# Weight-chunk bounds from TensorE column sums of the magnitude words, instead of a ScalarE pass with an accumulator

## The chip, the cores and the metric

The kernel runs on one core of one Trainium2 chip. The metric is the device time of one execution in microseconds (us); lower is better. Before the change, three runs gave 757.84, 759.58 and 761.88 us, median 759.58.

Names used below: TensorE (PE, with its weight loads as PEld), VectorE (DVE), ScalarE (ACT), GpSimd (POOL), SyncE (SP, which here only issues DMAs).

## The reference

Attention with a bias that a small network makes from positions, followed by a gated feed-forward block. Inputs are float32 for q, k, v and the bias network, and float64 for the three feed-forward weights.

```python
# B, H, S, D = 4, 8, 576, 64; d_model 512, d_ff 1536
scores = q @ k.T / sqrt(D) + bias(positions; w1, b1, w2)     # per batch and head
attn = softmax(scores)
x = (attn @ v) as [B * S, H * D]                             # 2304 x 512
out = ((x @ w_a) * (x @ w_b)) @ w_out
```

## The kernel before

**What runs.** For each batch, head pair and group of 256 query rows the kernel makes scores on TensorE (`qk`), adds the bias and takes the row minimum of the negated scores on VectorE (`soft1`, L518), takes exp with a row sum on ScalarE (L523), forms the reciprocal of the sum (GpSimd L567, VectorE L568), scales the rows on GpSimd (L573), transposes them on TensorE into PSUM (`turn`, L585), copies that to SBUF on ScalarE (L590, L595) and multiplies with v on TensorE (L535, L613). The feed-forward blocks (`moe_block`, L715, and `moe_out`, L764) run in 256-token pieces. The first feed-forward piece needs w_a and w_b as scaled pairs of float16 matrices, so in the first 160 us of the program attention tiles and weight preparation run side by side.

**Weight preparation.** w_a and w_b are cut into 12 chunks each of 128 x 512 float64 values: 24 chunks, taken in turn a, b, a, b, and handled in six groups of four. Step `s` of `wab_steps` (L318) does the following.

- `wab_conv` for chunk `s`: `w_unit` (L261) turns the two 32-bit halves of each float64 into a float32. ScalarE scales the upper half (L264); VectorE shifts (L266) and merges the lower half (L267), which leaves the *magnitude word*, the float32 without its sign, in `u`. `u` lies in the SBUF space where the float16 pair of that chunk will stand later (`w16t[:, f, j]`). VectorE then puts the sign in (L270) and the result goes to a float32 tile `wt`.
- `wab_size` for chunk `s-1` (L281): ScalarE passes over the signed float32 chunk with Abs and an accumulator, which leaves the sum of magnitudes of each of the 128 partitions in one column of `wm`. Its elementwise output lands in `w16t` and is overwritten later.
- Every fourth step, `pow2_down` (L75) turns the four columns of `wm` into four powers of two: a TensorE matmul against the identity brings them to four partitions (L77), VectorE takes the maximum over 128 elements (L79), clamps it (L80), keeps the exponent (L81) and spreads it on a diagonal (L85). Two steps later `pow2_up` broadcasts them to all partitions (TensorE L90, VectorE L92), and `wab_scale` makes reciprocals (L293, L294).
- `wab_parts` for chunk `s-7`: GpSimd scales the chunk (L304), ScalarE casts it to float16 (L307), GpSimd subtracts to get the lower part (L308).

**What sets the order.** TensorE's instructions run in the order of the code: the calls of `merge` interleave attention steps, weight steps and feed-forward steps, and a weight step's matmul stands where that step is called. The other engines' queues are ordered by a scheduler with a cost model; every engine works its queue in order. SP issues in order too: the load of a weight chunk (`wraw`, L258, three buffers in each of two pools) waits for the VectorE merge (L267) that frees its buffer, and the loads of bias rows and v behind it wait with it. PSUM banks matter at one place: the transposes of one tile (`tp`, one buffer) wait for ScalarE's copy of the tile before.

To keep the TensorE clock up in early stretches, `keep(n)` issues n matmuls whose result nobody reads (L845, 128 x 512 float16).

Of the kernel before, what the change touches and what calls it, by code (L numbers as in the profile page):

```python
# [8 lines left out]
F32 = mybir.dt.float32  # L9
F32R = mybir.dt.float32r  # L10
F16 = mybir.dt.float16
BF16 = mybir.dt.bfloat16
I32 = mybir.dt.int32
AF = mybir.ActivationFunctionType
ALU = mybir.AluOpType
AX = mybir.AxisListType
# [10 lines left out]
KC = DM // 128  # L27
# [25 lines left out]
def attention_moe(ctx, tc, q0d, q1d, kd, vd, idn, wp, wa, wb, wo, lsw, lg, rl, out):  # L53
    nc = tc.nc
# [14 lines left out]
    def pr_tile():  # L69
        if prp[0]:  # L70
            return prp[0].tile([128, 512], F32, tag="pr", name="pr", bufs=1)
        return mps.tile([128, 2 * TOK], F32, tag="ab", name="pr", bufs=3)


    def pow2_down(mx, n, tag):  # L75
        ps = pr_tile()
        nc.tensor.matmul(ps[0:n, 0:128], mx, tab["idn"], start=True, stop=True)  # L77
        m = wtp[1].tile([n, 1], F32, tag="p2m" + tag, name="p2m", bufs=2)
        nc.vector.reduce_max(out=m, in_=ps[0:n, 0:128], axis=AX.X)  # L79
        nc.vector.tensor_scalar(out=m, in0=m, scalar1=3.0e38, scalar2=2.0 ** -100, op0=ALU.min, op1=ALU.max)  # L80
        nc.vector.tensor_scalar(  # L81
            out=m.bitcast(I32), in0=m.bitcast(I32), scalar1=0x7F800000, scalar2=None, op0=ALU.bitwise_and
        )
        dg = wtp[1].tile([n, n], F32, tag="p2d" + tag, name="p2d", bufs=2)
        nc.vector.tensor_scalar(out=dg, in0=tab["idn"][0:n, 0:n], scalar1=m, scalar2=None, op0=ALU.mult)  # L85
        return dg

    def pow2_up(dg, n, tag):
        ps = pr_tile()
        nc.tensor.matmul(ps[:, 0:n], tab["one"][0:n, :], dg, start=True, stop=True)  # L90
        g = wtp[1].tile([128, n], F32, tag="p2g" + tag, name="p2g", bufs=2)
        nc.vector.tensor_copy(g, ps[:, 0:n])  # L92
        return g
# [9 lines left out]
    tab = {}  # L103
# [18 lines left out]
    def bias_windows(pool, tag):  # L122
        u = pool.tile([128, S], F32, tag=tag, name="u", bufs=1)
        nc.sync.dma_start(out=u, in_=lsw)
        return u
# [63 lines left out]
    @contextmanager  # L189
    def late():  # L190
        with ExitStack() as s:
            for x in (ttrs, exps, evs, pns):
                if x:
                    s.enter_context(tc.issue_after(x[-1].ins))
            yield
# [57 lines left out]
    last, wtp = [], [None, None]  # L253
# [21 lines left out]
    w16, wos, gpool = {}, {}, [None]  # L275
# [3 lines left out]
        with late():  # L279
            return w_unit(wt, raw, w16t[:, n // 2, n % 2].rearrange("p x k n -> p (x k n)").bitcast(I32))  # L280

    def wab_size(f, j, wf, m):
        nm = "ab"[j]
        w16[nm, f] = w16t[:, f, j]
        c = 2 * (f % 2) + j
        with late():
            nc.scalar.activation(
                w16[nm, f][:, 0], wf.rearrange("p (k n) -> p k n", k=KC), AF.Abs, accum_out=m[:, c:c + 1]
            )

    def wab_scale(p, m):
        rm = wtp[1].tile([128, 4], F32, tag="rm", name="rm", bufs=2)
        nc.vector.reciprocal(out=rm, in_=m)  # L293
# [4 lines left out]
        return rm  # L298

    def wab_parts(p, c, wf, rm):  # L300
        w = w16["ab"[c % 2], 2 * p + c // 2]
        wv = wf.rearrange("p (k n) -> p k n", k=KC)
        hi, lo = w[:, 0], w[:, 1]
        nc.gpsimd.tensor_scalar(  # L304
            out=wv, in0=wv, scalar1=rm[:, c:c + 1], scalar2=PS, op0=ALU.mult, op1=ALU.mult
        )
        nc.scalar.copy(hi, wv)  # L307
        nc.gpsimd.tensor_tensor(out=lo, in0=wv, in1=hi, op=ALU.subtract)  # L308
# [8 lines left out]

    def wab_steps(wt):  # L318
        np_ = FC // 2
        raws, wfs, ms, dgs, rms = {}, {}, {}, {}, {}  # L320

        def fetch(i):
            pool = wtp[0] if i % 2 else wt
            raws[i] = pool, w_load(pool, (wa, wb)[i % 2], i // 2)

        ahead = [0]

        def fetch_to(n):
            for i in range(ahead[0], min(n, 4 * np_)):
                fetch(i)  # L330
                ahead[0] = i + 1

        fetch_to(3)
        yield
        for s in range(4 * np_ + 7):
            p, c = divmod(s - 7, 4)
            if 0 <= p < np_:
                if c == 0:
                    rms[p] = wab_scale(p, pow2_up(dgs.pop(p), 4, "w"))
                with late():  # L340
                    wab_parts(p, c, wfs.pop(s - 7), rms[p])
            p, c = divmod(s - 5, 4)
            if 0 <= p < np_ and c == 0:
                dgs[p] = pow2_down(ms.pop(p), 4, "w")
            if 1 <= s <= 4 * np_:
                p, c = divmod(s - 1, 4)
                if c == 0:
                    ms[p] = wtp[1].tile([128, 4], F32, tag="wm", name="wm", bufs=2)
                wab_size(2 * p + c // 2, c % 2, wfs[s - 1], ms[p])
            if s < 4 * np_:  # L350
                wfs[s] = wab_conv(s, *raws.pop(s))
                fetch_to(s + 1 + min(6, 3 + s // 2))
            yield
# [474 lines left out]
    with tc.tile_pool(name="bg", bufs=1, side="right") as bg, tc.tile_pool(name="eq", bufs=1, space=PSUM) as eq, \  # L828
# [2 lines left out]
        bias_tables()  # L831
        tab["idn"] = cst.tile([128, 128], F32, name="idn")
        nc.scalar.dma_start(out=tab["idn"], in_=idn)
        tab["one"] = wtmp.tile([4, 128], F32, name="one")
        nc.vector.memset(tab["one"], 1.0)
        uls = bias_windows(att, "rk")
        bias_scale(uls)

# [154 lines left out]
```

## Time and profile before

| | us |
|---|---|
| runs: lowest, median, highest | 757.84, 759.58, 761.88 |
| span of the profiled execution | 760.0 |
| PE busy, share of the span | 704.6 (93%) |
| DVE busy | 498.8 (66%) |
| ACT busy | 446.3 (59%) |
| POOL busy | 329.1 (43%) |
| PE busy in 60 to 150 us (of 90) | 77.1 |
| PE busy after 240 us (of 520) | 497.3 |

The profiled execution has a span of 760.0 us from its first to its last instruction; no time of its own beside the span is listed, and the span lies 0.4 us above the median of the three runs.

How to read it: the shares of the first block are averages over the whole program. After about 165 us TensorE is nearly always busy. The weight preparation, which the change touches, lies between 20 and 161 us, and there the picture is mixed: TensorE waits, now and then, for ScalarE, for VectorE or for data. So the rows below are taken from that stretch, by stage and by wait, and the granted TensorE clock is read beside them (1.00 is 2.4 GHz, 0.50 is 1.2 GHz).

### The profile page before, as it was taken

The page shows a single profiled execution, that of the slowest core. Times are in us where ns is not written, and L with a number is a line of the kernel's source. Part 1 is how long each engine was busy: PE and PEld are TensorE (multiplying, and loading weights), DVE is VectorE, ACT ScalarE, POOL GpSimd, SP SyncE. Part 2 cuts the span into 40 slices and gives each one's busy share as a digit, 9 for nine tenths or more (in the row PEclk, how much of TensorE's full clock was granted, in tenths as well). Part 3 has the DMA queues.
Part 4 walks back from the last instruction along what each step waited for, and adds up shares of the span by engine and source line. Part 5 has one row for each costly group of instructions (what it writes and reads, how often), then busy time and mean ns, then how long its engine had stood idle before and what let it go on. Part 6 is the DMA issues. An engine that isn't in the chain of part 4 may idle for free.

```text
span 760.0 us, 15571 instructions
## 1 busy us (share of the span) xinstructions
PE 704.6 (93%) x5451; PEld 531.9 (70%) x5451; DVE 498.8 (66%) x1204; ACT 446.3 (59%) x1005; POOL 329.1 (43%) x477
## 2 busy tenths in 40 slices
PE   7778898899899999999889989999999999999997
PEld 2245465578787556687677768878778887888886
DVE  6767688849986578675788778878887772110200
ACT  6878887867875687754456456545655553422310
POOL 3437668855873133232545445524553452411200
PEclk9989999989999999999999999999999999999999
DMA  8898767477744888789999999999999974000001
GB/s 260 299 371 272 242 218 214 148 235 252 252 154 127 209 183 218 193 212 180 225 245 248 274 255 229 243 240 245 238 254 248 213 158 112 17 1 28 3 14 42
DMA packets 178163, 147.69 MB, mean 194 GB/s; under 512 B 125092, under 2 KB 138148, under 8 KB 178084
## 3 DMA queue, kind: packets, MB, share of 16 engines
q1 hardware_dynamic: 170928, 130.92, 68.2%
q10 hardware_dynamic: 5876, 10.93, 5.2%
q0 software_dynamic: 1280, 4.84, 1.8%
q8 instruction: 43, 0.70, 0.4%
q14 instruction: 36, 0.29, 0.1%
HBM read 101.15 MB, written 17.18 MB: 156 GB/s over the span
## 4 chain that ended last, share of the span: by engine, by line
PE 36%; issue 17%; DVE 15%; POOL 12%; ACT 10%; DMA 9%; SPq 1%; POOLq 0%; DVEq 0%; ACTq 0%
PE ab L715 15%; PE o L764 10%; POOL ph L553 5%; DMA bias<-bias_d 3%; POOL gl L740 3%; DMA pt<-ph 3%; DVE p L518 3%; PE pv L613 3%; PE psta L153 3%; DVE ph L555 2%; ACT p L523 2%; PE qk L490 2%; DVE w16t L267 2%; DVE wt L270 2%; POOL sm L567 2%
## 5 line engine op out<-in xcount | busy, mean ns | idle before, releaser
L715 PEld LDWEIGHTS <-w16t 128*128 128x128 f16 x2592 | 248.3, 98 | 47.2 <-issue 14.3
L715 PE MATMUL ab<-x,w16t 128*128 128x256 f16 x2304 | 273.2, 275 | 2.6 <-DVE g L725 1.0
L523 ACT ACTIVATE p<-p,mn 128x576 f32<-128x576 f32 x144 | 111.7, 776 | 138.7 <-DVE mn L518 117.4
L555 DVE SCALAR_TENSOR_TENSOR ph<-p,sm,ph 128x64 f16<-128x64 f32 x192 | 98.7, 554 | 34.1 <-POOL ph L553 32.0
L764 PE MATMUL o<-wos,gh 128*128 128x512 f32 x384 | 120.7, 395 | 0.0
L518 DVE CUSTOM_DVE_ANT_0 p<-qk,bias 128x576 f32<-128x576 f32 x144 | 107.7, 751 | 17.0 <-PE tp L585 5.6
L567 POOL TENSOR_SCALAR sm<-sm 128x1 f32<-128x1 f32 x144 | 42.1, 292 | 173.6 <-ACT p L523 169.3
L740 POOL TENSOR_TENSOR gl<-g,gh 128x256 fp32r<-128x256 f32 x96 | 75.1, 783 | 93.3 <-ACT gh L739 90.4
L553 POOL TENSOR_SCALAR ph<-p,sm 128x576 f16<-128x576 f32 x96 | 82.0, 854 | 52.5 <-DVE sm L568 39.7
L725 DVE SCALAR_TENSOR_TENSOR g<-ab,wv,asb 128x256 f32<-128x256 f32 x84 | 40.2, 479 | 73.0 <-ACT asb L723 73.0
L490 PE MATMUL qk<-ks,qs 128*128 128x288 f32 x384 | 72.9, 312 | 11.9 <-DVE mn L518 11.7
L764 PEld LDWEIGHTS o<-wos,gh 128*128 128x128 f32 x384 | 69.4, 188 | 16.0 <-issue 2.8
L764 PE MATMUL o<-wos,gl 128*128 128x512 f32 x192 | 75.0, 391 | 0.0
L490 PEld LDWEIGHTS qk<-ks,qs 128*128 128x128 f32 x384 | 55.8, 188 | 25.1 <-DVE mn L518 16.7
L739 ACT CAST gh<-g 128x256 fp32r<-128x256 f32 x96 | 38.3, 399 | 33.2 <-DVE g L725 32.8
L573 POOL TENSOR_SCALAR p<-p,sm 128x576 f32<-128x576 f32 x48 | 44.1, 920 | 28.5 <-DVE sm L568 23.9
L723 ACT ACTIVATE asb<-ab,wv 128x256 f32<-128x256 f32 x84 | 39.4, 469 | 27.6 <-PE ab L715 27.3
L568 DVE RECIPROCAL sm<-sm 128x1 f32<-128x1 f32 x144 | 23.1, 160 | 44.5 <-POOL sm L567 42.5
L407 DVE TENSOR_TENSOR ks<-rk,ks 64x576 fp32r<-64x576 f32 x48 | 44.9, 934 | 3.7 <-ACT ks L406 1.7
L613 PE MATMUL pv<-pt,vs 128*64 128x320 f16 (+1 forms) x560 | 41.8, 302 | 0.0
L585 PE MATMUL tp<-idn,p 128*128 128x128 f32 x240 | 37.1, 287 | 4.8 <-ACT ptf L590 4.0
L764 PEld LDWEIGHTS o<-wos,gl 128*128 128x128 f32 x192 | 36.0, 188 | 7.8
(102 smaller groups left out, 956.0 us busy)
## 6 DMA issues: line engine op xcount, KB each, us to landing
bias<-bias_d SPq DMA_DIRECT2D x128, 288.0 KB, 3.6
rv<-vd SPq DMA_DIRECT2D x32, 320.0 KB, 4.2
rk<-kd SPq DMA_DIRECT2D x24, 288.0 KB, 3.5
wraw<-wa SPq DMA_DIRECT2D x12, 512.0 KB, 7.0
wraw<-wb SPq DMA_DIRECT2D x12, 512.0 KB, 5.3
wraw<-wo SPq DMA_DIRECT2D x12, 512.0 KB, 4.5
bias_d<-bo ACTq DMA_DIRECT2D x20, 295.5 KB, 3.9
bias_d<-bo POOLq DMA_DIRECT2D x16, 295.5 KB, 7.0
```

Source lines behind the costliest of these rows:

```text
L407: nc.vector.tensor_tensor(out=ks[ol, j], in0=rk[sl], in1=ks[sl, j].bitcast(F32), op=ALU.subtract)
L490: nc.tensor.matmul(ps[:, hf, :HB], a, b[:, hf * HB:hf * HB + HB], start=(x == 0), stop=(x == len(prods) - 1))
L518: ttr = nc.vector.tensor_tensor_reduce(out=p.rearrange("p (a n) -> p a n", a=2), in0=ps[:, :, :HB], in1=bt.rearrange("p (a n) -> p a n", a=2),
L523: exps.append(nc.scalar.activation(p, p, AF.Exp, bias=mn, scale=-1.0, accum_out=sm))
L553: nc.gpsimd.tensor_scalar(out=ph[:, :S], in0=p, scalar1=rc, scalar2=1.0, op0=ALU.mult, op1=ALU.mult)
L555: ins = nc.vector.scalar_tensor_tensor(out=ph[:, o:o + c1 - c0], in0=p[:, c0:c1], scalar=rc, in1=ph[:, c0:c1], op0=ALU.mult, op1=ALU.subtract,
L567: nc.gpsimd.tensor_scalar(out=sm, in0=sm, scalar1=1e-9, scalar2=1.0 / (PS if u >= NF else 1.0), op0=ALU.add, op1=ALU.mult)
L573: nc.gpsimd.tensor_scalar(out=p, in0=p, scalar1=rc, scalar2=1.0, op0=ALU.mult, op1=ALU.mult)
L613: nc.tensor.matmul(ps[64 * j:64 * j + 64, o:o + N], v[:, j, :], p[:, j * N:j * N + N], start=(x == 0), stop=(x == len(prods) - 1),)
L715: nc.tensor.matmul(ab[:, j], w16[nm, f][:, pw, kk, :], xs[px][:, kk, :], start=(x % (3 * KC) == 0), stop=(x % (3 * KC) == 3 * KC - 1),)
L740: nc.gpsimd.tensor_tensor(out=gl, in0=g, in1=gh.bitcast(F32), op=ALU.subtract)
L764: nc.tensor.matmul(o, g[:, sl], wos[f][:, p], start=(f == 0 and x == 0), stop=(f == FC - 1 and x == 2))
```

## The change

ScalarE's pass over each chunk (`wab_size`) is gone, and with it `wm`. In its place `wab_bound`, called once for four chunks where `pow2_down` was called, reads the magnitude words that VectorE leaves in `w16t`: the upper 16 bits of each word, taken as bfloat16, are every second 16-bit element. Four matmuls, one for each chunk, multiply them with a 128 x 32 matrix of ones; each writes 32 rows of one PSUM bank, in which all 32 rows hold the chunk's 512 column sums. VectorE takes the maximum over 512 elements for 128 partitions at once, and the clamp, the exponent mask and the spreading follow on 128 partitions instead of 4 (`pow2_floor`). The spread uses a constant table `part` (1/32 in column c for the 32 partitions of chunk c), and `pow2_up` multiplies with a 128 x 128 matrix of ones. The bound is another number than before (largest column sum of truncated magnitudes, instead of the largest partition sum), but it is used in the same way. Three constants are made at the start, on VectorE.

```diff
+        return pow2_floor(m, tab["idn"][0:n, 0:n], tag)
+
+    def pow2_floor(m, rows, tag):
         nc.vector.tensor_scalar(out=m, in0=m, scalar1=3.0e38, scalar2=2.0 ** -100, op0=ALU.min, op1=ALU.max)
...
-        dg = wtp[1].tile([n, n], F32, tag="p2d" + tag, name="p2d", bufs=2)
-        nc.vector.tensor_scalar(out=dg, in0=tab["idn"][0:n, 0:n], scalar1=m, scalar2=None, op0=ALU.mult)
+        dg = wtp[1].tile(list(rows.shape), F32, tag="p2d" + tag, name="p2d", bufs=2)
+        nc.vector.tensor_scalar(out=dg, in0=rows, scalar1=m, scalar2=None, op0=ALU.mult)
         return dg
+
+    def wab_bound(p):
+        ps = pr_tile()
+        for c in range(4):
+            u = w16t[:, 2 * p + c // 2, c % 2].rearrange("p x k n -> p (x k n)").bitcast(BF16)
+            nc.tensor.matmul(
+                ps[32 * c:32 * c + 32], tab["ones"], u.rearrange("p (n w) -> p n w", w=2)[:, :, 1],
+                start=True, stop=True,
+            )
+        m = wtp[1].tile([128, 1], F32, tag="p2mw", name="p2m", bufs=2)
+        nc.vector.reduce_max(out=m, in_=ps, axis=AX.X)
+        return pow2_floor(m, tab["part"], "w")
...
-        nc.tensor.matmul(ps[:, 0:n], tab["one"][0:n, :], dg, start=True, stop=True)
+        nc.tensor.matmul(ps[:, 0:n], tab["one"][0:dg.shape[0], :], dg, start=True, stop=True)
...
-    def wab_size(f, j, wf, m):
-        nm = "ab"[j]
-        w16[nm, f] = w16t[:, f, j]
-        c = 2 * (f % 2) + j
-        with late():
-            nc.scalar.activation(
-                w16[nm, f][:, 0], wf.rearrange("p (k n) -> p k n", k=KC), AF.Abs, accum_out=m[:, c:c + 1]
-            )
-
...
-                dgs[p] = pow2_down(ms.pop(p), 4, "w")
-            if 1 <= s <= 4 * np_:
-                p, c = divmod(s - 1, 4)
-                if c == 0:
-                    ms[p] = wtp[1].tile([128, 4], F32, tag="wm", name="wm", bufs=2)
-                wab_size(2 * p + c // 2, c % 2, wfs[s - 1], ms[p])
+                dgs[p] = wab_bound(p)
...
+        tab["ones"] = wtmp.tile([128, 32], BF16, name="ones")
+        nc.vector.memset(tab["ones"], 1.0)
+        tab["part"] = wtmp.tile([128, 4], F32, name="part")
+        nc.vector.memset(tab["part"], 0.0)
+        for c in range(4):
+            nc.vector.memset(tab["part"][32 * c:32 * c + 32, c:c + 1], 1.0 / 32)
```

On TensorE the order stays, with the four matmuls where the one against the identity stood. On the other queues the scheduler moves things by a few places. Line numbers of the changed kernel are up to 15 higher or lower.

ScalarE's queue where the first feed-forward piece starts, about 91 to 99 us into the span. L307 casts a chunk, L287 is the pass that goes away, L264 starts the conversion of the next chunk, L523 is exp, L542 the output of a first tile, L595 the copy of a transposed tile. Before:

```order
L307 CAST w16t_66<-wt_654 128x512
L287 ACTIVATE w16t_66,wm_878<-wt_1047 128x512
L264 ACTIVATE wt_1150<-wraw_707 128x512
L523 ACTIVATE p_1159,sm_1161<-p_1159,mn_1160 128x576
L542 ACTIVATE x0_614<-pv_1127,vs0_452 128x128
L595 COPY ptw_1181<-tp_1175 128x5x128
L523 ACTIVATE p_1212,sm_1214<-p_1212,mn_1213 128x576
L307 CAST w16t_66<-wt_700 128x512
L287 ACTIVATE w16t_66,wm_1249<-wt_1150 128x512
L264 ACTIVATE wt_1251<-wraw_772 128x512
```

After (L313 is the cast, L279 the start of a conversion, L524 exp, L543 the output, L596 the copy):

```order
L313 CAST w16t_66<-wt_658 128x512
L279 ACTIVATE wt_1149<-wraw_710 128x512
L524 ACTIVATE p_1158,sm_1160<-p_1158,mn_1159 128x576
L543 ACTIVATE x0_617<-pv_1127,vs0_458 128x128
L596 COPY ptw_1180<-tp_1174 128x5x128
L524 ACTIVATE p_1211,sm_1213<-p_1211,mn_1212 128x576
L313 CAST w16t_66<-wt_703 128x512
L279 ACTIVATE wt_1251<-wraw_774 128x512
```

The two passes are out, and the start of the next conversion stands right behind the cast; the rest keeps its order.

VectorE's queue at about 146 to 151 us. L407 and L419 prepare k and q of a later unit, L518 is the pass over the scores that frees the PSUM bank for the next `qk`, L92 copies a broadcast bound. Before:

```order
L407 TENSOR_TENSOR ks_1873<-rk_1694,ks_1873 64x576 x2
L419 TENSOR_TENSOR qs_1878<-rq_1695,qs_1878 128x512
L518 ISA p_1939,mn_1940<-qk_1901,bias_1812 128x576
L518 ISA mn_1940 128x1
L92 COPY p2g_1916<-pr_1914 128x4
L568 RECIPROCAL sm_1870<-sm_1870 128x1
L725 SCALAR_TENSOR_TENSOR g_1898<-ab_1850,winv_65,asb_1896 128x256
```

After (L408, L420, L519 and L107 are the same four operations):

```order
L408 TENSOR_TENSOR ks_1869<-rk_1689,ks_1869 64x576 x2
L519 ISA p_1935,mn_1936<-qk_1897,bias_1805 128x576
L519 ISA mn_1936 128x1
L107 COPY p2g_1912<-pr_1910 128x4
L420 TENSOR_TENSOR qs_1874<-rq_1690,qs_1874 128x512
L726 SCALAR_TENSOR_TENSOR g_1894<-ab_1846,winv_65,asb_1892 128x256
```

The preparation of q has gone from ahead of the pass over the scores to behind it.

## Rows read from the trace of the kernel before

**Rows 1.** Busy time by stage: window, then its length, each engine, clock, DMA.

```profile
60.00:90.00 30.00, 24.60 (x205) 15.05 (x207) 22.00 (x63) 26.49 (x63) 20.33 (x29) 1.00 0.88 290
90.00:150.00 60.00, 52.46 (x405) 35.72 (x405) 49.03 (x119) 48.37 (x108) 46.23 (x56) 1.00 0.58 179
```

**Rows 2.** Groups by line and shape, 0 to 240 us: busy, mean ns, idle before.

```profile
L287 ACT ACTIVATE w16t<-wt 128x512 f16<-128x512 f32 x24 | 15.1, 629 | 5.5 <-DVE wt L270 5.4
L79 DVE TENSOR_REDUCE p2m<-pr 4x1 f32<-4x128 f32 x6 | 1.6, 270 | 0.4 <-PE pr L77 0.4
L725 DVE SCALAR_TENSOR_TENSOR g<-ab,winv,asb 128x256 f32<-128x256 f32 x12 | 5.7, 472 | 2.3 <-ACT asb L723 2.3
L518 DVE CUSTOM_DVE_ANT_0 p<-qk,bias 128x576 f32<-128x576 f32 x49 | 36.5, 749 | 11.6 <-PE tp L585 5.6 <-DMA bias<-bias_d 3.0 <-PE qk L504 3.0
```

**Rows 3.** TensorE in order of time; in brackets its idle time and releaser.

```profile
66.00 0.74 PE L585 MATMUL tp<-idn,p 128*128 128x128 f32 x5 [0.94 <-ACT ptf L590]
70.54 0.74 PE L585 MATMUL tp<-idn,p 128*128 128x128 f32 x5 [1.25 <-ACT ptf L590]
...
107.13 0.76 PE L481 MATMUL qk<-rkf,rqf 64*128 64x288 f32 x4 [1.47 <-DVE mn L518]
...
122.65 0.76 PE L481 MATMUL qk<-rkf,rqf 64*128 64x288 f32 x4 [1.35 <-DVE mn L518]
...
125.49 0.38 PE L77 MATMUL pr<-idn,wm 128*4 128x128 f32 x2 [1.39 <-ACT w16t L287]
...
140.75 0.38 PE L77 MATMUL pr<-idn,wm 128*4 128x128 f32 x2 [1.10 <-ACT w16t L287]
...
150.70 1.33 PE L481 MATMUL qk<-rkf,rqf 64*128 64x288 f32 x4 [2.46 <-DVE mn L518]
```

**Rows 4.** The chain that ended last: start, length, what.

```profile
68.64 0.62 ACT w16t L287 x2
...
92.53 0.62 ACT w16t L287 x2
...
98.55 0.62 ACT w16t L287 x2
```

**Rows 5.** VectorE in order of time, 137 to 151 us.

```profile
137.74 0.68 DVE L267 SCALAR_TENSOR_TENSOR w16t<-wraw,w16t 128x512 int32<-128x512 int32 x1
...
140.06 0.74 DVE L518 CUSTOM_DVE_ANT_0 p<-qk,bias 128x576 f32<-128x576 f32 x1
...
141.17 0.28 DVE L79 TENSOR_REDUCE p2m<-pr 4x1 f32<-4x128 f32 x1 [0.36 <-PE pr L77]
...
146.43 2.39 DVE L407 TENSOR_TENSOR ks<-rk,ks 64x576 fp32r<-64x576 f32 x2 [1.72 <-ACT ks L406]
148.84 1.12 DVE L419 TENSOR_TENSOR qs<-rq,qs 128x512 fp32r<-128x512 f32 x1
149.89 0.74 DVE L518 CUSTOM_DVE_ANT_0 p<-qk,bias 128x576 f32<-128x576 f32 x1
```

**Rows 6.** TensorE early: matmuls nobody reads (L845) and 32-row outputs (L153).

```profile
8.74 0.60 PE L845 MATMUL pr<-w16t 128*128 128x512 f16 x2
...
17.23 0.39 PE L845 MATMUL pr<-w16t 128*128 128x512 f16 x1
17.55 1.07 PE L153 MATMUL psta<-w16t,w2s 128*32 128x512 f32 x8
```

**Rows 7.** Busy time and granted clock in slices of 3 us, columns as Rows 1.

```profile
105.00:108.00 3.00, 1.53 (x13) 0.83 (x11) 3.00 (x10) 1.97 (x6) 0.07 (x1) 1.00 0.90 281
...
147.00:150.00 3.00, 1.24 (x12) 0.87 (x9) 2.94 (x4) 2.38 (x6) 2.92 (x3) 1.00 0.06 16
...
153.00:156.00 3.00, 3.00 (x16) 1.65 (x16) 0.85 (x3) 2.70 (x8) 2.84 (x6) 0.50 0.86 266
```

**Rows 8.** The same product with v, 20 matmuls, at 153 and at 233 us.

```profile
153.28 4.36 PE pv L613 x20
...
232.89 2.53 PE L613 MATMUL pv<-ptw,rvw 128*64 128x256 f32 x20
```

More of the change, by code (lines that the diff above doesn't have):

```diff
@@ L300, in wab_parts @@
     def wab_parts(p, c, wf, rm):
-        w = w16["ab"[c % 2], 2 * p + c // 2]
+        w = w16["ab"[c % 2], 2 * p + c // 2] = w16t[:, 2 * p + c // 2, c % 2]
         wv = wf.rearrange("p (k n) -> p k n", k=KC)
@@ L319, in wab_steps @@
         np_ = FC // 2
-        raws, wfs, ms, dgs, rms = {}, {}, {}, {}, {}
+        raws, wfs, dgs, rms = {}, {}, {}, {}
         def fetch(i):
@@ L833, in attention_moe @@
         nc.scalar.dma_start(out=tab["idn"], in_=idn)
-        tab["one"] = wtmp.tile([4, 128], F32, name="one")
+        tab["one"] = wtmp.tile([128, 128], F32, name="one")
         nc.vector.memset(tab["one"], 1.0)
+        tab["ones"] = wtmp.tile([128, 32], BF16, name="ones")
[4 more added lines that the diff above has]
+            nc.vector.memset(tab["part"][32 * c:32 * c + 32, c:c + 1], 1.0 / 32)
         uls = bias_windows(att, "rk")
```

## The prediction

> **What bounds the kernel now.** I read the busy time by stage first. After 165 us TensorE is busy almost throughout, and nothing of the change runs there, so the change can only shift that part as a block. Between 60 and 150 us [rows 1] TensorE is busy 24.6 of 30 us and then 52.5 of 60, ScalarE 26.5 and 48.4, VectorE 22.0 and 49.0, GpSimd 20.3 and 46.2. No engine is full; TensorE has 12.9 us of gaps, and the gain has to come out of these. Next I read TensorE in order of time, for the gaps and what ended them [rows 3]. There are three kinds: the transposes wait for ScalarE's copy of the tile before (0.94 and 1.25 us); the matmul that gathers the bounds waits for the very pass that the change removes (1.39 and 1.10); and the scores of the next tile wait for VectorE's pass L518 (1.47, 1.35 and 2.46). Third is the granted clock [rows 7]: it is 1.00 (2.4 GHz) in the slice with the 1.47 us gap, and 0.50 (1.2 GHz) in 153 to 156 us, after the slice 147 to 150 in which the gap of 2.46 us begins and TensorE was busy 1.24 of 3 us. Last comes the chain of waits, where the pass itself stands several times, each piece 0.62 long [rows 4].
>
> **What is removed: 24 ScalarE passes.** Each is 629 ns long [rows 2] and takes 0.62 us of the chain where it is on it [rows 4], so 24 x 0.62 = 14.9 us leave ScalarE's queue. Most of that is worth nothing where ScalarE would have waited anyway. Up to 60 us the chain runs mainly through the loading of bias rows, and I count 0 there. Gap by gap after that:
> - 66.00 and 70.54 [rows 3]: one pass stands in the same ScalarE queue ahead of each copy that TensorE waits for, so both gaps shorten by 0.62: 1.24 us.
> - 92.53 and 98.55 [rows 4]: two passes on the chain ahead of the stretch in which VectorE is full (3.00 of 3 us in 105 to 108 [rows 7]), which ends in the 1.47 us gap. At most 1.24; VectorE's own work is next late, so I take half, 0.6.
> - 125.49 [rows 3]: the wait ends altogether. The new matmuls need the magnitude words (L267), not the signed chunk (L270) and then the pass. 1.39 us.
> - 140.75 [rows 3]: the last L267 of that group ends at 137.74 + 0.68 = 138.4 [rows 5], before TensorE gets there at 139.65. But the next instruction on TensorE needs L518, which ends at 140.8 [rows 5]; VectorE is next late. It can start earlier by what 125.49 gave, which is counted already, so of 1.10 I take 0.5.
> - 150.70 [rows 3]: the scores wait for L518 at 149.89, which stands behind L419, 1.12 us long [rows 5]. In the new order of VectorE L419 stands behind L518: 1.12 us. The stretch started when ScalarE got to L406 (VectorE idle 1.72 us before L407 [rows 5]), and one pass less is ahead of that: 0.62. Of 2.46 us some 0.7 remain.
>
> Sum of the gaps: 1.24 + 0.6 + 1.39 + 0.5 + 1.12 + 0.62 = 5.5 us.
>
> **The clock.** With 0.7 us left of the 2.46, the gap is shorter than the one at 107.13 (1.47 [rows 3]), after which the clock stayed at 1.00 [rows 7]. I take it that the fall at 150 us does not come. Then the scores at 150.70 take 0.76 instead of 1.33 [rows 3] and the product with v 2.53 instead of 4.36 [rows 8]: 0.57 + 1.83 = 2.4 us. Transposes between them, also at half rate, are left out of the sum.
>
> **What is added on TensorE.** Six times four matmuls of 512 columns come in place of a pair that takes 0.38 us [rows 3]. One 128 x 512 float16 matmul takes 0.39 us alone, and a second adds 0.60 - 0.39 = 0.21 [rows 6]. The four write different 32-row strips, as L153 does: there eight matmuls of 512 columns took 1.07 us, where one after the other at 0.21 they would need 0.39 + 7 x 0.21 = 1.86 us [rows 6]. So strips overlap, and one group costs from 0.39 (all four at once) to 0.39 + 3 x 0.21 = 1.02 (one after the other). I take the former, since L153 is the nearest row. Going over to strips costs something: the matmul at 17.23 is followed by L153 after 0.32 us and not 0.21 [rows 6], 0.11 more. A group is then 0.50 against 0.38, and four groups lie where TensorE is nearly full: 4 x 0.12 = 0.5 us; with the four in series 4 x 0.75 = 3.0. Reading every second 16-bit element is shown by no row; I count nothing for it, and the series case covers a reading at half the rate.
>
> The page "TensorEngine Tiling (Array Packing)" of the Trainium skill, section Key Properties, speaks against the change here: changing the tiling mode drains TensorE. By that rule each group pays on entering and on leaving, and at the 0.11 us of the row (an estimate) six groups pay 12 x 0.11 = 1.3 us instead of the 0.5 above. The trace shows the price going in; the sum does not hang on the rule.
>
> **What is added on VectorE.** The maximum goes over 512 elements instead of 128, six times. Before it took 270 ns; 256 elements from PSUM took 472 in L725, 576 took 749 in L518 [rows 2], which is 0.87 ns an element. From L79 upward that is 270 + 384 x 0.87 = 0.60 us, from L725 upward 472 + 256 x 0.87 = 0.69; I take 0.65, 0.38 more each, 2.3 in all. Behind it VectorE is usually idle: at 141.17 it had waited for TensorE [rows 5], and the bound is not needed for some 10 us. One of the six, at 73 us, lies where VectorE is busy without a break, so I charge 0.4 us. The clamp, the mask and the spreading have as many elements a partition as before, and the constants are made while the first loads are under way: 0. The wait ahead of the new matmuls is one for VectorE; queued behind it on TensorE are transposes, scores or feed-forward matmuls, and at the two places where L77 waited this wait does not come, by the L267 times above. SP and GpSimd issue the same DMAs and passes; a weight load waits for L267, and gets free earlier, not later.
>
> **Sum.** 760.0 - 5.5 - 2.4 + 0.5 + 0.4 = 753.0 us against the span of the profiled execution, which lies 0.4 us above the median of the runs; I keep **753**.
>
> **The rivals.**
> - *A, the clock falls all the same.* The gap at 150 us shrinks, but what is left of it and of the stretch before still takes the clock down. For it: the busy times of the slice that lost the clock and of the one that kept it are not far apart (1.24 and 1.53 us [rows 7]), and the gap is not the only pause there. 753.0 + 2.4 = 755.4.
> - *B, ScalarE was not the one that mattered.* VectorE and GpSimd are as busy as ScalarE in 90 to 150 us [rows 1] and are next late everywhere but where TensorE waited for the pass and where the order changed. Then only 1.39 + 0.5 + 1.12 remain, against the costs of 0.9, and the clock still falls, since 1.3 us of gap is left: 760.0 - 3.0 + 0.9 = 757.9.
> - *C, the four matmuls run one after the other.* 3.0 instead of 0.5: 755.5. Against it speak the L153 rows [rows 6].
> - *D, slower.* VectorE is the bound, as in 105 to 108 us (3.00 of 3 us [rows 7]), and its longer maximum delays L518: all six count, 2.3 us, TensorE's 0.5 comes on top, and the freed ScalarE gives nothing. It decides where a wait of 1.47 us, which left the clock up, becomes one like the 2.46 us that took it down [rows 3, 7]: one further fall costs another 2.4. 760.0 + 2.3 + 0.5 + 2.4 = 765.2. Against it: the maxima I could place stand where VectorE had just been idle.
>
> **Chances and range.** Forecast 0.42, A 0.20, B 0.20, C 0.06, D 0.12. A measurement of this kernel can tell about 0.5%, 3.8 us, from no change. Faster by more than that means below 755.8: the forecast nearly whole and half of A and C, since they lie on the edge, 0.54. Slower by more is D nearly whole, 0.11. Within 0.5%: 0.35. The lower end of the range is all seven waits of [rows 3] gone (9.96 us) with the clock (2.4): 760.0 - 12.4 = 747.6, so 747; the upper end takes in B and a span without any gain, 761. D lies outside (0.12), and 0.08 is left for a gain or a loss by something not seen here.
>
> **What would show it.** Right: no wait of the new matmuls for ScalarE or VectorE over 0.2 us; a group of four within 0.5 us; the reduction near 0.65 us; the gaps for ScalarE's copies at 66 and 70 us down by 0.6; the scores after the k preparation waiting under 1 us and the clock at 1.00 over 150 to 158 us; the rest of the program as long as before, so that what the stretch to 165 us gains is what the span gains. Wrong: TensorE's waits for L518 grown by as much as the others shrank (B or D); a clock fall at a new place; four matmuls that start 0.2 us apart (C); or later stretches, the last weight matrix at 165 to 240 us above all, giving the gain back because bias loads or VectorE arrive no earlier there.

## The result, and the profile after

The changed kernel takes 764.27 us (median; before, on the same chip, 760.13): a ratio of 1.0069, 95% interval 1.0048 to 1.0090. Side by side a second time it gave 1.0070 (1.0038 to 1.0103); one of those 12 executions, with a granted clock of 0.655, took 986.91 us and is left out of this ratio. So the forecast of 753 us is wrong in sign, and 764 lies outside the range. The two traces shown differ less (spans of 760.0 and 760.5 us), because the one of before is the longest execution of its kernel in that comparison (761.88 us) and the one after is among the shortest of its own (762.63); a second trace of before has a span of 756.6. One trace therefore says where something happens, and only medians say what it is worth.

Stage by stage in the changed kernel, columns as in [rows 1]:

```profile
60.00:90.00 30.00, 25.54 (x203) 16.19 (x204) 23.26 (x60) 23.87 (x53) 20.61 (x29) 0.94 0.88 276
90.00:150.00 60.00, 52.51 (x406) 35.50 (x406) 49.05 (x118) 37.46 (x76) 42.19 (x52) 0.97 0.59 184
```

ScalarE has lost 2.6 us of work in the first stage and 10.9 in the second. TensorE's busy time has not fallen, and its clock is at 0.94 and 0.97 where it was at 1.00. The removed work left the queue; nothing came of it.

The groups that answer [rows 2], 0 to 240 us, in the same columns:

```profile
L100 DVE TENSOR_REDUCE p2m<-pr 128x1 f32<-128x512 f32 x6 | 4.1, 682 | 0.4 <-PE pr L95 0.4
L519 DVE CUSTOM_DVE_ANT_0 p<-qk,bias 128x576 f32<-128x576 f32 x48 | 35.8, 750 | 10.2 <-PE tp L586 4.8 <-PE qk L505 3.0 <-DMA bias<-bias_d 2.3
```

The new reduction L100 takes 682 ns (estimated at 0.65 us), 0.41 more than L79 [rows 2]. TensorE in order of time, answering [rows 3]; in brackets idle time and releaser:

```profile
67.81 0.90 PE L586 MATMUL tp<-idn,p 128*128 128x128 f32 x5 [2.71 <-ACT ptf L591]
...
99.59 0.41 PE L95 MATMUL pr<-w16t,ones 128*32 128x512 bf16 x4
99.93 0.76 PE L482 MATMUL qk<-rkf,rqf 64*128 64x288 f32 x4
...
108.91 0.76 PE L482 MATMUL qk<-rkf,rqf 64*128 64x288 f32 x4 [1.64 <-DVE mn L519]
...
125.03 0.76 PE L482 MATMUL qk<-rkf,rqf 64*128 64x288 f32 x4 [2.20 <-DVE mn L519]
...
142.51 0.41 PE L95 MATMUL pr<-w16t,ones 128*32 128x512 bf16 x4 [0.65 <-DVE p2g L107]
144.37 0.76 PE L482 MATMUL qk<-rkf,rqf 64*128 64x288 f32 x4 [1.45 <-DVE mn L519]
...
153.18 0.97 PE L482 MATMUL qk<-rkf,rqf 64*128 64x288 f32 x4 [1.90 <-DVE mn L519]
```

The waits for the removed pass (1.39 and 1.10 in [rows 3]) are gone. But the wait for a copy at 66 us has become 2.71 where it was 0.94, and, of the waits shown here, every one for VectorE's score pass except the last is longer: 1.47 became 1.64, 1.35 became 2.20, and 1.45 at 144 us had no counterpart.

The 2.71 us is followed back through the four queues. First VectorE, before (upper fence) and after (lower):

```profile
63.23 0.16 DVE L92 COPY p2g<-pr 128x4 f32<-128x4 f32 x1 [0.86 <-PE pr L90]
63.43 0.18 DVE L293 RECIPROCAL rm<-p2g 128x4 f32<-128x4 f32 x1
63.52 0.20 DVE L294 TENSOR_SCALAR winv<-p2g,vi 128x4 f32<-128x4 f32 x1
63.63 0.42 DVE L266 TENSOR_SCALAR w16t<-wt 128x512 int32<-128x512 int32 x1
64.08 1.06 DVE L267 SCALAR_TENSOR_TENSOR w16t<-wraw,w16t 128x512 int32<-128x512 int32 x1
```

```profile
63.11 0.47 DVE L281 TENSOR_SCALAR w16t<-wt 128x512 int32<-128x512 int32 x1
63.62 0.69 DVE L282 SCALAR_TENSOR_TENSOR w16t<-wraw,w16t 128x512 int32<-128x512 int32 x1
64.39 0.16 DVE L569 RECIPROCAL sm<-sm 128x1 f32<-128x1 f32 x1
64.47 0.67 DVE L285 SCALAR_TENSOR_TENSOR wt<-wt,w16t 128x512 int32<-128x512 int32 x1
65.06 0.15 DVE L107 COPY p2g<-pr 128x4 f32<-128x4 f32 x1
65.13 0.34 DVE L544 SCALAR_TENSOR_TENSOR x<-pv,vs,x 128x128 f16<-128x128 f32 x1
65.39 0.17 DVE L299 RECIPROCAL rm<-p2g 128x4 f32<-128x4 f32 x1
```

Before, VectorE stood idle for 0.86 us, took the bound (L92) and then converted a chunk. After, the conversion (L281, L282, L285) stands in that hole and the bound (L107, L299) behind it, so the scale comes at 65.39 and not at 63.43. Then GpSimd and ScalarE after:

```profile
64.72 1.04 POOL L574 TENSOR_SCALAR p<-p,sm 128x576 f32<-128x576 f32 x1 [0.36 <-DVE sm L569]
65.74 1.36 POOL L310 TENSOR_SCALAR wt<-wt,rm 128x512 f32<-128x512 f32 x2
```

```profile
66.46 0.62 ACT L313 CAST w16t<-wt 128x512 f16<-128x512 f32 x1 [2.13 <-POOL wt L310]
66.98 0.69 ACT L591 COPY ptf<-tp 128x640 f32<-128x640 f32 x1
```

On GpSimd the scaling L310 starts at 65.74, where L304 started at 63.70 before. The scale came late, and in GpSimd's new order a normalisation (L574) stands ahead of the scaling: it ends when the scale has been there for some 0.2 us. ScalarE's cast L313 waits 2.13 us for the scaling, and behind the cast in ScalarE's queue stands the copy L591 that TensorE's transposes wait for. ScalarE, which was to be relieved, is idle and blocked.

The clock there, slices of 3 us of the changed kernel (columns as in [rows 1], the clock third from the end):

```profile
63.00:66.00 3.00, 2.10 (x14) 1.46 (x14) 2.88 (x11) 1.20 (x4) 1.78 (x4) 1.00 0.93 240
66.00:69.00 3.00, 1.19 (x9) 0.90 (x11) 0.69 (x4) 2.54 (x6) 2.45 (x4) 0.87 1.00 331
69.00:72.00 3.00, 3.00 (x26) 2.21 (x24) 2.93 (x5) 2.24 (x5) 2.92 (x3) 0.56 1.04 249
```

It falls to its lower level (1.2 GHz) behind the wait, at a place where it stayed at 1.00 before.

### The profile page after: what moved, and what is told of

Read it like the earlier page. It is cut to its first block, busy times and chain, and to the rows that moved or that the text cites. A ratio compares the mean times of both kernels' runs of the same rounds, so it can differ in the third digit from the quotient of the medians.

```text
span 760.5 us, 15556 instructions
## 1 busy us (share of the span) xinstructions
PE 705.9 (93%) x5463; PEld 533.8 (70%) x5463; DVE 505.2 (66%) x1210; ACT 432.1 (57%) x957; POOL 330.2 (43%) x477
## 4 chain that ended last, share of the span: by engine, by line
PE 37%; issue 16%; DVE 15%; POOL 13%; DMA 9%; ACT 8%; SPq 1%; POOLq 0%; DVEq 0%; ACTq 0%
PE ab L716 14%; PE o L765 11%; POOL ph L554 5%; POOL gl L741 4%; DMA pt<-ph 3%; DVE p L519 3%; PE psta L168 3%; DMA bias<-bias_d 3%; DVE ph L556 3%; PE pv L614 2%; DVE ks L408 2%; ACT p L524 2%; POOL sm L568 2%; PE pr L852 2%; PE qk L491 2%
## 5 line engine op out<-in xcount | busy, mean ns | idle before, releaser
L524 ACT ACTIVATE p<-p,mn 128x576 f32<-128x576 f32 x144 | 111.7, 775 | 148.4 <-DVE mn L519 128.6
L519 DVE CUSTOM_DVE_ANT_0 p<-qk,bias 128x576 f32<-128x576 f32 x144 | 107.6, 750 | 16.9 <-PE tp L586 6.6
L574 POOL TENSOR_SCALAR p<-p,sm 128x576 f32<-128x576 f32 x48 | 45.8, 954 | 22.2 <-DVE sm L569 18.4
L408 DVE TENSOR_TENSOR ks<-rk,ks 64x576 fp32r<-64x576 f32 x48 | 45.0, 938 | 3.6 <-ACT ks L407 1.7
```

What stands on the lines that cost most here:

```text
L408: nc.vector.tensor_tensor(out=ks[ol, j], in0=rk[sl], in1=ks[sl, j].bitcast(F32), op=ALU.subtract)
L519: ttr = nc.vector.tensor_tensor_reduce(out=p.rearrange("p (a n) -> p a n", a=2), in0=ps[:, :, :HB], in1=bt.rearrange("p (a n) -> p a n", a=2),
L524: exps.append(nc.scalar.activation(p, p, AF.Exp, bias=mn, scale=-1.0, accum_out=sm))
L574: nc.gpsimd.tensor_scalar(out=p, in0=p, scalar1=rc, scalar2=1.0, op0=ALU.mult, op1=ALU.mult)
```

## The experiments

Two theories were set up. **Theory 1:** the loss is the new order of the in-order queues. **Theory 2:** it is the new work, VectorE's reductions first. The order was taken apart from the work by a helper that ties consecutive instructions of ScalarE, VectorE, GpSimd and SyncE's DMA queue by order-only edges, in an order read from the built program of another kernel (a table of places, left out here). In the kernels with such a table line numbers are 15 larger than in the kernel they are made from (15 to 25 in the filled ones).

```diff
+def put_in_order(tc, left_out=()):
+    ...
+        for a, b in zip(places, places[1:]):
+            tc.add_manual_dep(mine[b], mine[a].name, no_sync, reason="order")
...
     run(moe_out(gs, main_rows(0, 0), mps))
+    put_in_order(tc, added)
```

**The kernel before again.**

> The kernel before, unchanged, looked at once more: a second trace of it. The first trace had a span of 760.0 us, at the slow end of its times. Every theory expects 757 to 762 us of device time. If the new trace's clock falls lie where they did (51, 150, 201, 365, 440 us after the start of the span), falls at 67.8 and 125.9 us belong to the changed kernel; if they wander, they can't be read from one trace each.

758.59 us. The clock fell at 45, 148, 199 and 434 us and not at 68 or 126.

**New work, old order** (the changed kernel and the table of the kernel before).

> The changed kernel, but the instructions on ScalarE, VectorE, GpSimd and SyncE's DMA queue stand in the order of the kernel before (without the 24 removed passes), held there by order-only edges. All of the new work is in it and none of the new order. Theory 1, the loss is from the new order of the queues: faster than before, about 755 us, ratio 0.993, with no clock fall at 67.8 or 125.9 us. Theory 2, the loss is the six reductions over 512 columns on VectorE (682 ns each where there were 270 ns) or TensorE's groups of four: slower than before as the changed kernel was, about 764 us, ratio 1.005.

1.0036 (1.0017 to 1.0055): about half the loss goes with the order alone, but no gain appears.

**Passes put back.** The pass is added to the changed kernel, with no order imposed:

```diff
+            if 1 <= s <= 4 * np_:
+                with late():
+                    nc.scalar.activation(
+                        wtp[1].tile([128, 512], mybir.dt.uint8, tag="wj", name="wj", bufs=1), wfs[s - 1], AF.Abs,
+                        accum_out=wtp[1].tile([128, 1], F32, tag="wm", name="wm", bufs=2),
+                    )
```

> The changed kernel with a ScalarE pass of magnitudes over each chunk put back where it stood (its sums go to a tile that nobody reads), so ScalarE has all of its old work and VectorE and TensorE all of their new; left to itself the order comes out nearly as before (0 places differ on GpSimd, 2 of 837 on ScalarE, 24 of 1060 on VectorE, 4 of 483 on SyncE). Theory 1 (order): about 760 to 761 us, ratio 1.000 to 1.002. Theory 2 (the new work itself): no better than the changed kernel, 764 us or more, ratio 1.006 or more.

1.0011 (0.9985 to 1.0036). More work, and not slower than without it: the order that comes with the passes is worth at least what they cost.

**Old work, new order** (the kernel before and the table of the changed kernel).

> The kernel before, its passes of magnitudes included, with all other instructions of ScalarE, VectorE, GpSimd and SyncE in the order of the changed kernel. None of the new work is in it. Theory 1 (order): as slow as the changed kernel or slower, since the passes are still there, 764 to 768 us, ratio 1.006 to 1.011. Theory 2 (the new work): as before, 760 us, ratio 1.000.

1.0120 (1.0089 to 1.0152), 767.25 us, from four executions. None of the new work is in it. Theory 1 holds for the larger part.

**Passes cut, old order**, then **passes cut, new order**, which complete the comparison of order and work.

```diff
-                w16[nm, f][:, 0], wf.rearrange("p (k n) -> p k n", k=KC), AF.Abs, accum_out=m[:, c:c + 1]
+                w16[nm, f][:, 0, :, 0:1], wf.rearrange("p (k n) -> p k n", k=KC)[:, :, 0:1], AF.Abs, scale=128.0, accum_out=m[:, c:c + 1]
```

> The kernel before, each of its 24 passes of magnitudes cut from 512 columns to 4 (scaled by 128, so that the bound stays of the same size; it leaves out the other columns), all queues in the order of the kernel before. The old chain of the bound, some 10 us of ScalarE gone, and nothing else. Theory A, as the prediction has it: the passes stood on TensorE's way at seven places, so 5 to 8 us go: about 753 us, ratio 0.990 to 0.993. Theory B: without them the wait passes to the next that is late, VectorE's score passes, and nothing is gained: 757.5 to 759.5 us, ratio 0.998 to 1.001.

0.9996 (0.9963 to 1.0028): theory B. What TensorE waits for with the passes cut (waits of TensorE, 45 to 165 us: in total, times, longest):

```profile
PE qk L496 <- DVE mn L533: 5.6, 4, 2.7
PE tp L600 <- ACT ptf L605: 5.0, 7, 0.9
PE pr L92 <- ACT w16t L302: 2.0, 2, 1.0
```

The same three rows in the second trace of the kernel before read:

```profile
PE qk L481 <- DVE mn L518: 5.3, 3, 2.5
PE tp L585 <- ACT ptf L590: 4.3, 5, 1.3
PE pr L77 <- ACT w16t L287: 2.5, 2, 1.4
```

The waits ascribed to the pass shrink little (0.96 and 1.00 us, where [rows 3] has 1.39 and 1.10), although it now takes 0.22 us. It was named as releaser because it ended last. At 141 us it had itself waited for VectorE's conversion, as most of its idle time in [rows 2] does (5.4 of 5.5 us behind L270). At 126 us it stood in ScalarE's queue behind a cast that waited for GpSimd:

```profile
125.51 0.62 ACT L322 CAST w16t<-wt 128x512 f16<-128x512 f32 x1 [0.68 <-POOL wt L319]
126.05 0.22 ACT L302 ACTIVATE w16t<-wt 128x4 f16<-128x4 f32 x1
```

The trace of before has the same chain ahead of 125.49: the cast waited 0.38 us for GpSimd's scaling, and this 0.92 us for VectorE's reciprocal (L293). At the copies it is alike. Ahead of the transposes at 66.00 the cast waited 0.16 us for GpSimd; with the pass ahead of it 0.41 us shorter that wait is 0.58, and TensorE's stays at 0.94. Time taken out of ScalarE's queue became ScalarE's wait.

> The kernel before with its passes of magnitudes cut from 512 columns to 4 (scaled by 128; the other columns are left out), all queues in the order of the changed kernel: the new order without the new work and without the old. In the old order the same work gave 0.9996 (0.9963 to 1.0028), granted clock 0.985. Theory 1, the order makes the loss by taking the clock down more often: 1.004 to 1.007 and a mean granted clock of about 0.979. Theory 2, the new work makes it: 1.000 and about 0.985.

1.0048 (1.0020 to 1.0077). With the old work cut short and none of the new, the new order alone makes most of the loss.

**Short reductions**, in the old order and in the changed kernel's own.

```diff
-        nc.vector.reduce_max(out=m, in_=ps, axis=AX.X)
+        nc.vector.reduce_max(out=m, in_=ps[:, 0:128], axis=AX.X)
```

> The changed kernel in the order of the kernel before, with the six reductions over 128 of the 512 columns (it leaves out three quarters of the column sums): 270 ns for each where there were 682. With the full reductions this order gave 1.0036 (1.0017 to 1.0055). Theory 2a, VectorE's longer reductions make that 0.36%: 1.000 or less. Theory 2b, they lie beside other work and something else in the new work costs it (TensorE's groups, the bound that now hangs on VectorE's conversions): 1.003 again.

1.0000 (0.9970 to 1.0030) against 1.0036 with the full ones.

> The changed kernel in its own order, with the six reductions over 128 of the 512 columns (three quarters of the column sums are left out). The changed kernel gave 1.0069 (1.0048 to 1.009). Theory 1, the order of the queues: nearly all of it stays, 1.005 to 1.007. Theory 2, the reductions on a full VectorE: about 1.001 to 1.003.

1.0050 (1.0011 to 1.0089) against 1.0069. Both times the short ones are faster, by 1.4 to 2.7 us; six times 0.41 is 2.5. The intervals overlap, so this points to the reductions costing nearly their full length and does not show it.

**Where in the order?** Two tables put together at 90 and 94 us.

> The changed kernel; what began before 90 us stands in the order of the kernel before, the rest in the order of the changed kernel. If the new order costs its time ahead of 90 us (casts at 66 us behind a late reciprocal, TensorE's wait of 2.7 us and the fall at 68 us), this is near the 1.0036 of the old order, clock 0.985. If it is behind (the waits for score passes at 107, 123 and 143 us, the falls at 126 and 153), it is near the 1.0069 of the changed kernel, clock 0.979.

1.0020 (0.9991 to 1.0048).

> The reverse: the changed kernel, what began before 94 us in its own order, the rest in the order of the kernel before. Loss ahead of 90 us: 1.0069 and clock 0.979. Loss behind: 1.0036 and clock 0.985. If both stages take part, this and the one before both lie between.

1.0052 (1.0024 to 1.0080). Both point to the early stage: 1.0052 with the new order there, 1.0020 without it. The intervals overlap, so this alone does not settle it; the longer waits at 109, 125 and 144 us cost little that can be measured.

**One place.** In the changed kernel's own order, three entries of VectorE's list and two of GpSimd's are moved:

```diff
 VectorE, new line numbers
+L122 p2g, L314 rm, L315 winv
 L296, L297, L584, L300        (one conversion unit and a reciprocal)
-L122 p2g, (L559 x), L314 rm, L315 winv
 GpSimd
+L325 scale, L325 scale
 L583, L589                    (one normalisation)
-L325 scale, L325 scale
```

> The changed kernel in its own order but for one place: the copy of the new bound out of PSUM and the reciprocal and product behind it stand on VectorE ahead of the conversion unit of 64 us, as in the kernel before, and the two scalings on GpSimd that wait for them stand ahead of one normalisation. If the late reciprocal is what holds ScalarE's casts, and these the copies that TensorE's transposes wait for, the wait of 2.71 us at 65 us falls to about 1.4 and the clock fall at 68 us is gone in most executions: 762 to 763 us, 1.004 to 1.005, clock about 0.982. If not, 1.007.

1.0019 (0.9993 to 1.0045). Since that interval nearly touches the changed kernel's, both were run once more on one chip:

> The changed kernel, unchanged, beside the next one on the same chip. By the first comparison 1.0048 to 1.009, about 4 to 6 us over before.

> The kernel with the scales of the bound first at the one place of 64 us, a second time, so that it stands beside the changed kernel on one chip. If the late reciprocal there carries most of the loss, it is 2 to 4 us faster than the changed kernel, 1.000 to 1.0045 against before. If the first result was chance, both agree within 1 us.

1.0070 (1.0038 to 1.0103) and 1.0023 (0.9991 to 1.0055). The difference is 0.0050 in the first comparison and 0.0047 in the second, 3.6 to 3.8 us from one place. Each interval is about as wide as the difference; what carries it is that both comparisons agree. The place is one on two queues: what VectorE's three entries and GpSimd's two give each by itself was not tried. All engines in order of time there (second trace of this kernel), and then the clock:

```profile
65.52 0.16 DVE L122 COPY p2g<-pr 128x4 f32<-128x4 f32 x1
65.71 0.18 DVE L314 RECIPROCAL rm<-p2g 128x4 f32<-128x4 f32 x1
...
65.98 2.00 POOL L325 TENSOR_SCALAR wt<-wt,rm 128x512 f32<-128x512 f32 x2 [0.19 <-DVE rm L314]
...
66.92 0.62 ACT L328 CAST w16t<-wt 128x512 f16<-128x512 f32 x1
67.62 0.69 ACT L606 COPY ptf<-tp 128x640 f32<-128x640 f32 x1
...
68.46 0.74 PE L601 MATMUL tp<-idn,p 128*128 128x128 f32 x5 [0.87 <-ACT ptf L606]
```

```profile
66.00:69.00 3.00, 2.13 (x16) 1.43 (x13) 2.10 (x5) 2.13 (x5) 2.55 (x4) 1.00 0.97 250
69.00:72.00 3.00, 2.33 (x24) 1.34 (x22) 1.78 (x6) 1.98 (x5) 2.45 (x4) 1.00 0.95 320
```

The cast no longer waits, the transposes wait 0.87 and not 2.71, and the clock stays up. A fall that begins between 62 and 69 us is in all six traces with the changed kernel's order ahead of 90 us. It is in none of the seven with the order of before there, nor in the two with this place mended. In the six the cast waits 2.12 to 2.33 us for GpSimd; in the nine others it waits at most 0.58 us. In one of the six (passes cut, new order) the fall begins at 62 us, ahead of the wait, so the wait is not its only cause. The wait gives 1.84 of the 3.6 us; that the rest is the fall is a difference, not a measurement of its own.

**New work, score passes first.** If VectorE's waits were the bound, putting 20 score passes ahead of conversion steps should pay:

```diff
 VectorE, at 121 us (20 such places)
+L534 score pass
 L297, L296, L300, L297, L644, L584, L296, L300
-L534 score pass
```

> The changed kernel in the order of the kernel before, but on VectorE 20 score passes between 40 and 170 us stand ahead of the conversion steps (and of the key and query parts at 149 and 167 us) that began after their product was ready in the trace of that order; the three other queues as they were. If TensorE's waits for the score passes (1.7, 1.6, 1.0 and 2.9 us at 104, 120, 139 and 147 us) and the clock falls behind them set the end of this stage, some 5 us go against the order it is made from: about 755 us, ratio 0.995 to 0.998. If the conversions are needed as urgently (the bound, the casts and the weights behind them become late), it is no faster: 1.003 or more.

1.0124 (1.0076 to 1.0172): a miss. TensorE's longest waits became these:

```profile
PE pv L551 <- DVE x L559: 7.4, 3, 3.0
PE tp L601 <- ACT ptf L606: 3.5, 4, 1.8
PE pr L110 <- DVE p2g L122: 2.6, 2, 1.7
```

The score passes jumped over short steps too (L559, L122) for which TensorE waits as well. TensorE waits 1.77 us for a copy ahead of 66.16 and 2.55 us for L559 ahead of 69.44, and the clock falls at 67 us here, too.

**The scale a step early.** An edit in the source instead of a table, in the changed kernel and as a control in the one before:

```diff
-                if c == 0:
-                    rms[p] = wab_scale(p, pow2_up(dgs.pop(p), 4, "w"))
                 with late():
                     wab_parts(p, c, wfs.pop(s - 7), rms[p])
+            p, c = divmod(s - 6, 4)
+            if 0 <= p < np_ and c == 0:
+                rms[p] = wab_scale(p, pow2_up(dgs.pop(p), 4, "w"))
```

> The changed kernel with one edit in the source and no order imposed: the step that turns the new bound into scales (the matmul, the copy out of PSUM, the reciprocal, the product) is issued one step earlier, ahead of a conversion unit instead of with the first cast. Six of six reciprocals then stand 1 or 2 score passes earlier on VectorE. If the late reciprocal carries the loss, this gives what moving it by hand gave, 1.000 to 1.003, clock about 0.984. If it was the one place by chance and the reshuffled order brings other waits, 1.005 or more.

1.0079 (1.0048 to 1.0109): a miss. The matmul that spreads the bound now comes to TensorE before VectorE has made it:

```profile
106.84 0.39 PE L105 MATMUL pr<-p2d,one 128*128 128x4 f32 x2 [2.42 <-DVE p2d L88]
```

> The same edit made to the kernel before, passes of magnitudes and all. If the reciprocal there is early enough already, nothing changes: 0.999 to 1.002. If an early scale is worth something by itself, 0.995 to 0.998, and it would have to be taken off what the same edit gives in the changed kernel.

1.0016 (0.9996 to 1.0036): worth nothing there.

**Filled waits.** Matmuls that nobody reads ahead of tiles 31 and 41:

```diff
+    def fill(n):
+        if n in (31, 41):
+            ps, x = tpp.tile([128, 5, 128], F32, tag="tp", name="fl", bufs=1), tab["idn"].bitcast(BF16)
+            for _ in range(16):
+                nc.tensor.matmul(
+                    ps[:, 0:2].rearrange("p a n -> p (a n)"), x[:, 0:128], x, start=True, stop=True
+                )
...
+                fill(n + 1)
                 qk(n + 1)
```

> The kernel before in its own order, with 16 matmuls of 128x256 that nobody reads put on TensorE's queue ahead of the products of tiles 31 and 41, where TensorE waits 2.5 and 2.6 us (at 145.6 and 194.8 us) and the clock falls behind it (147.6 us, 6.8 long, and 198.8 us, 3.4 long). If a fall costs the 2.4 us that the prediction gave it, the two cost 3 to 5 us and this gives 754 to 756 us, ratio 0.994 to 0.996, clock 0.991 to 0.993. If it costs what the executions so far show (370 us for the whole of the mean clock, so 0.0067 is 2.5 us), 0.997. If the matmuls stand in the way of TensorE's own work, 1.000 or slower.

0.9996 (0.9977 to 1.0016). In the trace the falls at 148 and 199 us are gone, and the clock is 1.00 from 127 to 361 us:

```profile
147.53 1.91 PE L481 MATMUL fl<-idn 128*128 128x256 bf16 x16 [1.21 <-ACT ptw L618]
149.37 0.76 PE L504 MATMUL qk<-rkf,rqf 64*128 64x288 f32 x4
150.05 0.77 PE L608 MATMUL tp<-idn,p 128*128 128x128 f32 x5
150.75 2.53 PE L636 MATMUL pv<-ptw,rvw 128*64 128x256 f32 x20
```

The filling starts late, because its PSUM tile waits for ScalarE. Scores, transposes and product took 1.33, 1.33 and 4.34 us in the second trace of before: 2.94 us less for the same rows, but they begin 1.33 us later, and of the rest the medians show nothing that can be told from zero. The same trace has a fall at 123 to 127 us, behind a wait of 1.39 us; both traces of the kernel before have this wait, too, and kept 1.00 there. So falls also move, and what one costs a typical execution stays open.

> The changed kernel with the scale a step early, in that kernel's own order, and the same 16 matmuls ahead of tiles 31 and 41. If the falls there cost the same in both kernels, it gains on the unfilled one what the filled kernel before gains on its own: 2 to 4 us. Should the removal of the passes be worth anything once both the late scale and these falls are out of the way, it is faster than the filled kernel before; by theory B (VectorE sets the pace) it is not.

1.0117 (1.0090 to 1.0144) against 1.0079 unfilled (the intervals overlap): filling pays nothing that shows in this kernel either, and the part of the expectation on the passes can't be read from it, since the early scale was itself a loss.

No version beats the kernel before.

## Why the prediction was wrong, point by point

- **The step that failed: the order was taken as that of before, but for the places named.** "One pass stands in the same ScalarE queue ahead of each copy that TensorE waits for, so both gaps shorten by 0.62" and "a weight load waits for L267, and gets free earlier, not later" count removed time in fixed queues. The scheduler made a new order throughout the stage, and at one place it put a conversion unit ahead of the bound's last steps on VectorE and a normalisation ahead of the scaling on GpSimd. That place costs 3.6 to 3.8 us. The order of both kernels shows it; the prediction read that order where it hoped for a gain and not here.
- **The step that failed beside it: 5.5 us of gaps put down to the pass.** In the old order, with some 10 of its 15 us gone, nothing is gained (0.9996, 0.9963 to 1.0028).
- **66.00 and 70.54, 1.24 us forecast.** The wait at 66 became 2.71 us, since ScalarE's cast blocked the copy. With the order as before and the passes cut, the waits for copies come to 5.0 us in total (4.0 and 4.3 in the two traces of before): no gain. That one pass stands ahead of each copy was true of the queue; at 66.00 the copy's start hung on a cast that waits for GpSimd (0.16 us, then 0.58).
- **125.49 and 140.75, 1.9 us forecast.** The waits for the pass did end. VectorE was next late at both: ahead of the first place 1.35 became 2.20, and at the second 0.65 and 1.45 stand for 1.10. Added up, 3.84 us of waits became 4.30. The 0.65 is the new matmuls' own, for VectorE's copy L107, where the prediction had no wait of theirs for VectorE. "VectorE is next late" was said of 140.75 alone; it held at both. Cutting the pass to 0.22 us left 1.0 of each wait: it was VectorE's at 140.75, and at 125.49 that of a cast held by GpSimd.
- **92.53 and 98.55, 0.6 us:** nothing; 1.47 became 1.64.
- **150.70, 1.74 us and the clock's 2.4.** L420 did move behind the score pass, but L408 started at 149.60 (146.43 in [rows 5]) and took 2.72 us, so 1.90 us of wait remained and the clock fell all the same, as rival A has it. The 0.62 us for one pass less ahead of it did not come: VectorE waits 1.68 us there, and waited 1.72 before:

```profile
149.60 2.72 DVE L408 TENSOR_TENSOR ks<-rk,ks 64x576 fp32r<-64x576 f32 x2 [1.68 <-ACT ks L407]
152.35 0.76 DVE L519 CUSTOM_DVE_ANT_0 p<-qk,bias 128x576 f32<-128x576 f32 x1
```

- **TensorE's added 0.5 us: too much, on the safe side.** Four matmuls take 0.41 us, and the next matmul starts 0.34 us after the group (99.59 to 99.93). Behind the pair of L77 it started 0.31 us after (98.17 to 98.48), so a group costs 0.03 us more and not 0.12. Rival C is out.
- The rule of the Trainium skill, "TensorEngine Tiling (Array Packing)", Key Properties, that a change of the tiling mode drains TensorE, adds nothing that shows here: the group at 99.59 and the scores behind it have no idle time of their own in the rows. The 1.3 us worked out by it are not seen.
- **VectorE's added 0.4 us: the size was right, the cover is open.** 682 ns was estimated at 0.65 us. "The bound is not needed for some 10 us" charged one of six; the short reductions point to 1.4 to 2.7 us, nearly all six, but do not show it.
- **Rivals.** B had the right mechanism for the removal: in the old order it gains nothing (0.9996), less than B's 3.0 us. D came nearest in time (765.2 against 764.27), with VectorE as the bound and a new clock fall, but partly by luck: it put the cause into the longer maximum, for which the runs point to 1.4 to 2.7 us, and it did not have the order.

The range failed because its upper end took in "a span without any gain" and no loss from the order.

## What to carry to other kernels

When a change takes work out of a scheduled program, read the new order at every place where engines wait, not only where a gain is hoped for: a short step on which a chain of three queues hangs may now stand behind a long one that is merely ready. The engine that a wait names is the one that came last; ask what that one was waiting for, and what stood ahead of it in its queue, before its work is counted as the wait's price. Test removal and order apart: cutting the work down in the old order tells at once whether it was worth anything.

## What the runs showed of the hardware

- The mean granted clock, averaged over the executions of a comparison, was 0.979 to 0.980 for the changed kernel and 0.984 to 0.987 for the one before. But it does not rank kernels: with the passes put back it was 0.990 at a ratio of 1.0011, with the scale a step early 0.985 at 1.0079, and filled waits (0.989) gained no time that could be measured. So the mean clock does not give the price of a fall.
- Four matmuls that write different 32-row strips and read every second 16-bit element ran side by side: each took 0.40 us (median of 24), all four 0.41, against 0.39 for one alone that reads every element [rows 6]. This way of reading cost nothing that shows.
- A conversion step of VectorE (L267) took 1.06 us at 64.08 in the trace of before, beside a scaling on GpSimd, and the same step (L282) 0.69 us at 63.62 after, when GpSimd had little to do (0.20 us at 64.16; its scaling came at 65.74). This was not tried by itself. The scaling before:

```profile
63.70 2.00 POOL L304 TENSOR_SCALAR wt<-wt,rm 128x512 f32<-128x512 f32 x2 [0.42 <-DVE rm L293]
```
